# Loading a projection's first weights by whole rows, with the first activation pieces of one row each

## The chip, the cores and the metric

One core of one Trainium2 chip. The metric is the device time of one execution in microseconds (us). Matmuls run on TensorE (PE, with its weight loads shown as PEld), elementwise work on VectorE (DVE) and ScalarE (ACT), and SyncE (SP) issues most of the DMA transfers. In every execution listed with its span, the device time was about 1.7 us over the span of the profile (first to last instruction), so spans and times can be compared by differences.

All runs here count as "fast" (within 1.5% of the fastest of the same kernel).

## The reference

Two attention blocks read the same x (2048 tokens, 1024 channels) and are mixed by a gate. Only the first lines of block A matter here:

```
qkv = x @ A_wqkv                       # 1024 -> 3 x 1024
phi = lambda t: where(t > 0, t + 1, exp(t)) + 1e-6
pq, pk = phi(q), phi(k)                # the kernel computes pk first
... linear attention A, windowed attention B, out = g * a + (1 - g) * b
```

## The kernel before

The first stage computes the keys of A. Their weights are the middle 1024 columns of A_wqkv: 1024 rows, or 8 "row tiles" of 128 rows (index `kt`). x is transposed by DMA into `xT`, also by row tile. A "row" below means such a row tile. A matmul takes 128 tokens of one row of xT and 512 columns of the weights. The first four token tiles (t = 0 to 3) times two column halves fill eight accumulator tiles in PSUM (the kernel calls them banks) and are accumulated together, so that work can begin when the first rows have arrived.

```python
WkA = [wpool.tile([P, KT, 512], BF16, name=f"WkA{h}", tag="wa") for h in range(2)]

def load_xT(k, t0, t1):          # rows 2k and 2k+1
    nc.sync.dma_start_transpose(out=xT[:, 2*k:2*k+2, t0*P:t1*P],
                                in_=rows(x, t0*P, t1*P)[:, 2*k*P:(2*k+2)*P])
def load_wk(eng, k, h):          # rows 2k and 2k+1, half the columns: 1 KB runs
    eng.dma_start(out=WkA[h][:, 2*k:2*k+2, :], in_=A_wqkv[...])

load_wk(nc.scalar, 0, 0)
nc.scalar.activation(out=first_act[:], in_=ones[:, 0:1], func=ACT.Exp)
load_wk(nc.scalar, 0, 1)
load_xT(0, 0, 2)
load_xT(0, 2, 4)
for k in range(1, 4):
    load_wk(nc.sync, k, 0)
    load_xT(k, 0, 4)
    load_wk(nc.sync, k, 1)
# ... (cut: xT for token tiles 4 to 15, xrow, the later weights)

warm_up(37)                      # 37 matmuls on constants, 128 columns each
first = [bank_k(i) for i in range(8)]
for k in range(4):
    for half in range(2):
        for t in range(4):
            for kt in (2*k, 2*k + 1):
                project(first[4*half + t], t, kt, half)
            if k == 3:
                phi(work, pk[:, t, half*512:(half+1)*512], first[4*half + t])
# ... (cut: token tiles 4 to 15, eight rows at a time; the second stage, g_ps; all the rest)
```

Note when weights are needed. Within a group of two rows the first 8 matmuls use half 0 alone, so the group's second piece of weights is needed 8 matmuls after its first.

The softmax here doesn't subtract the row's maximum and nothing guards it: scores larger than these inputs give would overflow.

## Time and profile before

| | before |
|---|---|
| median of 6 runs | 473.12 us (472.91 to 473.46) |
| span of the profiled run | 471.7 us |
| TensorE busy | 467.6 us, 99% |
| last warm-up matmul issued | 4.63 us |
| first projection matmul | 5.39 us |
| second stage's first matmul | 60.92 us |

The page's part 1 (busy time and share of each engine) and part 4 (the chain of work that ended last), kernel before:

```profile
PE 467.6 (99%) x5765; PEld 251.1 (53%) x5765; DVE 278.4 (59%) x602; ACT 168.7 (36%) x272; POOL 15.3 (3%) x30
...
PE 98%; DMA 1%; DVE 0%; issue 0%; DVEq 0%
```

TensorE is the bottleneck nearly everywhere; the one other thing on the chain is the first x piece.

The timeline of TensorE over the first 14 us, kernel before (start, duration, engine, line, what, count, and in brackets the idle time before it and what ended it):

```profile
0.84 4.10 PE L175 MATMUL warm<-const-bfloat16-1.0 128*128 128x128 bf16 x37 [0.84 <-PEq L641]
5.39 8.86 PE L169 MATMUL pk_ps<-WkA,xT 128*128 128x512 bf16 x39 [0.45 <-DMA xT<-in_A_x_dram]
```

From 5.39 on, TensorE is never without work. Ends of matmuls are modelled, so I count gaps between starts: the last warm-up is issued at 4.63, the warm-ups are 0.107 us apart, so the array could have taken a new matmul at 4.74 and stood still until 5.39.

Busy time in stretches of 2 us, kernel before (stretch, length, then busy us and number of instructions of each engine, granted clock, DMA share, GB/s):

```profile
4.00:6.00 2.00, 1.55 (x11) 0.95 (x10) 0.00 (x0) 0.00 (x0) 0.00 (x0) 1.00 1.06 248
6.00:8.00 2.00, 2.00 (x10) 0.88 (x9) 0.00 (x0) 0.00 (x0) 0.00 (x0) 1.00 1.01 219
8.00:10.00 2.00, 2.00 (x11) 0.90 (x10) 0.00 (x0) 0.00 (x0) 0.64 (x2) 1.00 1.16 271
```

The number to read is the count of PE instructions. At full clock these matmuls start 0.216 us apart, so 2 us hold 9 or 10 starts.

### The profile page before, as it was taken

What the parts mean: (1) busy time and instruction counts of PE and PEld (TensorE: products, weight loads), DVE (VectorE), ACT (ScalarE), POOL (GpSimd) and SP (SyncE); (2) the same over time, 40 slices, a digit from 0 to 9 for tenths busy, and PEclk for the clock granted to TensorE, in tenths of its full rate; (3) what the DMA queues carried; (4) which work ended last, traced back from release to release, by engine and by line L of the source; (5) the groups of instructions that cost most, each with busy time, mean ns of one, the idle gap of its engine ahead of it and who ended that gap; (6) DMA issues with size and microseconds to landing.
All of it is one profiled execution on the core that took longest, in us unless ns stands there. A gap on an engine that the chain in (4) does not pass through costs nothing.

```text
span 471.7 us, 13176 instructions
## 1 busy us (share of the span) xinstructions
PE 467.6 (99%) x5765; PEld 251.1 (53%) x5765; DVE 278.4 (59%) x602; ACT 168.7 (36%) x272; POOL 15.3 (3%) x30
## 2 busy tenths in 40 slices
PE   8999999999999999999999999999999999999997
PEld 5444444445444444445677777777764444444444
DVE  0586689990329999999567676767670049800000
ACT  1343321112443333333555555555551134221121
POOL 3300000500000000000000000000000000000000
PEclk9999999999999999999999999999999999999999
DMA  8999970000643233627326364632563913221101
GB/s 220 193 246 374 348 248 0 0 1 1 213 134 108 92 142 128 156 96 248 103 56 100 71 91 96 91 93 63 93 173 67 227 64 79 69 54 45 35 33 46
DMA packets 98732, 55.40 MB, mean 117 GB/s; under 512 B 70130, under 2 KB 90610, under 8 KB 98674
## 3 DMA queue, kind: packets, MB, share of 16 engines
q1 hardware_dynamic: 93378, 49.87, 41.1%
q10 hardware_dynamic: 5296, 4.69, 2.9%
q8 instruction: 45, 0.74, 0.7%
q14 instruction: 13, 0.11, 0.1%
HBM read 26.10 MB, written 15.86 MB: 89 GB/s over the span
## 4 chain that ended last, share of the span: by engine, by line
PE 98%; DMA 1%; DVE 0%; issue 0%; DVEq 0%
PE q_ps L388 27%; PE d_ps L592 12%; PE p_ps L295 12%; PE pk_ps L169 12%; PE g_ps L220 12%; PE e_ps L592 12%; PE p_ps L331 9%; PE po L467 2%; PE s2b L445 2%; DMA xT<-in_A_x_dram 1%; PE kv_ps L240 0%; PE w_ps L283 0%; DVE osb L599 0%; DVEq L599 0%
## 5 line engine op out<-in xcount | busy, mean ns | idle before, releaser
L388 PE MATMUL q_ps<-xT,WqB 64*64 64x512 bf16 x1024 | 69.7, 377 | 0.0
L388 PE MATMUL q_ps<-xT,WkB 64*64 64x512 bf16 x1024 | 69.0, 376 | 0.0
L156 DVE TENSOR_SCALAR e<-e 128x512 f32<-128x512 f32 x64 | 27.1, 423 | 64.0 <-ACT e L155 64.0
L295 PE MATMUL p_ps<-WvB,xT 128*128 128x512 bf16 x256 | 57.9, 379 | 0.0
L169 PE MATMUL pk_ps<-WkA,xT 128*128 128x512 bf16 x256 | 55.7, 380 | 0.4 <-DMA xT<-in_A_x_dram 0.4
L220 PE MATMUL g_ps<-pk,xrow 128*128 128x512 bf16 x256 | 55.4, 379 | 0.0
L450 ACT ACTIVATE PT<-s2b 128x928 bf16<-128x928 f32 (+4 forms) x40 | 34.1, 854 | 45.5 <-PE s2b L445 45.5
L452 DVE TENSOR_TENSOR PT<-PT,mask 128x928 bf16<-128x928 bf16 (+4 forms) x40 | 23.6, 589 | 36.2 <-ACT PT L450 36.2
L331 PE MATMUL p_ps<-WqA,xT 128*128 128x512 bf16 x192 | 43.4, 379 | 0.0
L592 PEld LDWEIGHTS <-pqT 128*128 128x128 bf16 x272 | 26.0, 98 | 29.8 <-issue 0.4
L592 PEld LDWEIGHTS <-OBT 128*128 128x128 bf16 x272 | 26.0, 98 | 29.4
L169 PEld LDWEIGHTS <-xT 128*128 128x128 bf16 x256 | 25.0, 98 | 30.9 <-DMA xT<-in_A_x_dram 0.7
L220 PEld LDWEIGHTS <-xrow 128*128 128x128 bf16 x256 | 25.0, 98 | 30.2
L295 PEld LDWEIGHTS <-xT 128*128 128x128 bf16 x256 | 24.6, 98 | 30.0 <-issue 0.9
L388 PEld LDWEIGHTS <-WkB 64*64 64x64 bf16 x1024 | 34.0, 107 | 11.6 <-issue 0.4
L388 PEld LDWEIGHTS <-WqB 64*64 64x64 bf16 x1024 | 32.5, 107 | 11.1 <-issue 1.0
L599 DVE TENSOR_SCALAR osb<-e_ps,omg 128x128 bf16<-128x128 f32 x1 | 0.4, 351 | 57.6 <-PE e_ps L592 57.6
L155 ACT ACTIVATE e<-pk_ps 128x512 f32<-128x512 f32 x32 | 18.9, 597 | 40.5 <-PE pk_ps L169 36.3
L300 ACT CAST tmp<-p_ps 128x512 bf16<-128x512 f32 x32 | 18.7, 589 | 37.1 <-PE p_ps L295 32.3
L592 PE MATMUL d_ps<-WoA,pqT 128*128 128x512 bf16 (+1 forms) x136 | 30.9, 370 | 0.0
L331 PEld LDWEIGHTS <-xT 128*128 128x128 bf16 x192 | 18.8, 98 | 22.6
L592 PE MATMUL d_ps<-WoB,OBT 128*128 128x512 bf16 (+1 forms) x136 | 30.8, 370 | 0.0
(63 smaller groups left out, 530.3 us busy)
## 6 DMA issues: line engine op xcount, KB each, us to landing
vd<-tmp SPq DMA_DIRECT2D x16, 264.0 KB
xrow<-in_A_x_dram SPq DMA_DIRECT2D x4, 1024.0 KB
out_dram<-osb ACTq DMA_DIRECT2D x31, 128.0 KB
pqd<-tmp SPq DMA_DIRECT2D x12, 256.0 KB
WvA<-in_A_wqkv_dram SPq DMA_DIRECT2D x2, 1024.0 KB
WoA<-in_A_wo_dram SPq DMA_DIRECT2D x2, 1024.0 KB
WvB<-in_B_wqkv_dram SPq DMA_DIRECT2D x2, 1024.0 KB
WqA<-in_A_wqkv_dram SPq DMA_DIRECT2D x2, 1024.0 KB
```

What stands on the lines that cost most here:

```text
L155: nc.scalar.activation(out=e[:], in_=pj[:], func=ACT.Exp)
L156: nc.vector.tensor_scalar(out=e[:], in0=e[:], scalar1=1.0, scalar2=1e-6, op0=ALU.min, op1=ALU.add)
L169: nc.tensor.matmul(pj[:], lhsT=xT[:, kt, t * P:(t + 1) * P], rhs=WkA[half][:, kt, :], start=(kt == 0), stop=(kt == KT - 1))
L220: nc.tensor.matmul(pj[:], lhsT=xrow[:, t, kt * P:(kt + 1) * P], rhs=pk[:, t, half * 512:(half + 1) * 512], start=(t == 0), stop=(t == NB - 1))
L295: nc.tensor.matmul(st["pj"][:], lhsT=xT[:, kt, t * P:(t + 1) * P], rhs=WvB[half][:, kt, :], start=(kt == 0), stop=(kt == KT - 1))
L300: nc.scalar.copy(out=v[:, half * 16:(half + 1) * 16, 0:Dh], in_=st["pj"][:].rearrange("p (h e) -> p h e", h=16))
L331: nc.tensor.matmul(st["pj"][:], lhsT=xT[:, kt, t * P:(t + 1) * P], rhs=WqA[half][:, kt, :], start=(kt == 0), stop=(kt == KT - 1))
L388: nc.tensor.matmul(banks[o][64 * j:64 * j + 64, :], lhsT=lhsT(r, kt, j), rhs=rhs(r, kt), start=first and kt == 0, stop=kt == KT - 1, skip_ ...
L445: nc.tensor.matmul(s2b[64 * par:64 * par + 64, pair, :, o:o + w], lhsT=kts[c][r, par, k0:k0 + 64], rhs=qz[r, :, par, q0 % 512:q0 % 512 + w ...
L450: nc.scalar.activation(out=pt[:, :, 0:W_], in_=s2b[:].rearrange("p a b s -> p (a b) s")[:, :, 0:W_], func=ACT.Exp, scale=SCALE)
L452: nc.vector.tensor_tensor(out=pt[:, :, 0:W_], in0=pt[:, :, 0:W_], in1=mask[:, None, base:base + W_].broadcast_to([P, 4, W_]), op=ALU.mult)
L592: nc.tensor.matmul(st["ps"][:, 0:n], lhsT=lhsT, rhs=W[c0 // 512][:, c, c0 % 512:c0 % 512 + n], start=(side == 0 and c == 0), stop=(side == ...
```

## The change

Its intent: longer runs (2 KB for 1 KB) for the key weights, smaller first pieces of x in rows, and an order of matmuls that starts with one row over all eight banks. Core of the diff (the same edit of WqA's and lw's tiles is cut; TensorE's, VectorE's and GpSimd's instructions keep their order and number, apart from the rows' order in the first 64 matmuls):

```diff
-    WkA = [wpool.tile([P, KT, 512], BF16, name=f"WkA{h}", tag="wa") for h in range(2)]
+    WkA = wide.tile([P, KT, D], BF16, name="WkA", tag="wa")
...
+    def load_wk(eng, kt):
+        eng.dma_start(out=WkA[:, kt, :], in_=A_wqkv[kt * P:(kt + 1) * P, D:2 * D])
...
-        load_wk(nc.scalar, 0, 0)
-        first_act = consts.tile([P, 1], BF16, name="first_act")
-        nc.scalar.activation(out=first_act[:], in_=ones[:, 0:1], func=ACT.Exp)
-        load_wk(nc.scalar, 0, 1)
-        load_xT(0, 0, 2)
-        load_xT(0, 2, 4)
-        for k in range(1, 4):
-            load_wk(nc.sync, k, 0)
-            load_xT(k, 0, 4)
-            load_wk(nc.sync, k, 1)
+        load_wk(nc.scalar, 0)
+        load_wk(nc.scalar, 1)
+        load_xT(0, 1, 0, 4)
+        load_xT(1, 1, 0, 4)
+        for kt in range(2, KT, 2):
+            load_wk(nc.sync, kt)
+            load_xT(kt, 2, 0, 4)
+            load_wk(nc.sync, kt + 1)
...
-            for k in range(4):
+            for kts_ in ((0,), (1,), (2, 3), (4, 5), (6, 7)):
                 for half in range(2):
                     for t in range(4):
-                        for kt in (2 * k, 2 * k + 1):
+                        for kt in kts_:
                             project(first[4 * half + t], t, kt, half)
-                        if k == 3:
+                        if kts_[-1] == KT - 1:
```

More of the change, by code (lines that the diff above doesn't have):

```diff
@@ L71 @@
     wpool = ctx.enter_context(tc.tile_pool(name="wpool", bufs=2))
+    wide = ctx.enter_context(tc.tile_pool(name="wide", bufs=1))
     dram = ctx.enter_context(tc.tile_pool(name="dram", bufs=1, space=bass.MemoryType.DRAM))
@@ L89, in load_rows, with load_xT @@
         eng.dma_start(out=xrow[:, t0:t1, :], in_=rows(x, t0 * P, t1 * P).rearrange("(t p) d -> p t d", p=P))
-    WkA = [wpool.tile([P, KT, 512], BF16, name=f"WkA{h}", tag="wa") for h in range(2)]
-    def load_xT(k, t0, t1):
-        nc.sync.dma_start_transpose(out=xT[:, 2 * k:2 * k + 2, t0 * P:t1 * P],
-                                    in_=rows(x, t0 * P, t1 * P)[:, 2 * k * P:(2 * k + 2) * P])
-    def load_wk(eng, k, h):
-        eng.dma_start(out=WkA[h][:, 2 * k:2 * k + 2, :],
-                      in_=A_wqkv[2 * k * P:(2 * k + 2) * P, D + 512 * h:D + 512 * h + 512]
-                      .rearrange("(kt p) n -> p kt n", p=P))
+    WkA = wide.tile([P, KT, D], BF16, name="WkA", tag="wa")
+    def load_xT(kt, n, t0, t1):
+        nc.sync.dma_start_transpose(out=xT[:, kt:kt + n, t0 * P:t1 * P],
+                                    in_=rows(x, t0 * P, t1 * P)[:, kt * P:(kt + n) * P])
+    def load_wk(eng, kt):
+        eng.dma_start(out=WkA[:, kt, :], in_=A_wqkv[kt * P:(kt + 1) * P, D:2 * D])
     ones = nc.const_aps.tensor(1.0, [P, P], BF16)
     with tc.manual_schedule(engines={SP, mybir.EngineType.Activation}):
-        load_wk(nc.scalar, 0, 0)
-        first_act = consts.tile([P, 1], BF16, name="first_act")
-        nc.scalar.activation(out=first_act[:], in_=ones[:, 0:1], func=ACT.Exp)
-        load_wk(nc.scalar, 0, 1)
-        load_xT(0, 0, 2)
-        load_xT(0, 2, 4)
-        for k in range(1, 4):
-            load_wk(nc.sync, k, 0)
-            load_xT(k, 0, 4)
-            load_wk(nc.sync, k, 1)
+        load_wk(nc.scalar, 0)
[6 more added lines that the diff above has]
+            load_wk(nc.sync, kt + 1)
         for t in range(4, NB):
@@ L122 @@
         WvB = load_w("WvB", B_wqkv, 2 * D, "wc")
-    WqA = load_w("WqA", A_wqkv, 0, "wa")
+    WqA = wide.tile([P, KT, D], BF16, name="WqA", tag="wa")
+    for h in range(2):
+        nc.sync.dma_start(out=WqA[:, 4 * h:4 * h + 4, :],
+                          in_=A_wqkv[512 * h:512 * h + 512, 0:D].rearrange("(kt p) n -> p kt n", p=P))
     mask = consts.tile([P, S // 2], BF16, name="mask")
@@ L168, in project @@
             def project(pj, t, kt, half):
-                nc.tensor.matmul(pj[:], lhsT=xT[:, kt, t * P:(t + 1) * P], rhs=WkA[half][:, kt, :],
+                nc.tensor.matmul(pj[:], lhsT=xT[:, kt, t * P:(t + 1) * P], rhs=WkA[:, kt, half * 512:half * 512 + 512],
                                  start=(kt == 0), stop=(kt == KT - 1))
@@ L330, in mm @@
                         st["pj"] = bank()
-                    nc.tensor.matmul(st["pj"][:], lhsT=xT[:, kt, t * P:(t + 1) * P], rhs=WqA[half][:, kt, :],
+                    nc.tensor.matmul(st["pj"][:], lhsT=xT[:, kt, t * P:(t + 1) * P], rhs=WqA[:, kt, half * 512:half * 512 + 512],
                                      start=(kt == 0), stop=(kt == KT - 1))
@@ L544 @@
             fw = wpool.tile([P, 2, D], F32, name="fw", tag="wc")
-            lw = wpool.tile([P, 4, D], BF16, name="lw", tag="wa")
+            lw = wide.tile([P, 4, D], BF16, name="lw", tag="wa")
             def qa_output(t, half):
@@ L551, in rhs @@
                 def rhs(r, kt):
-                    return WqA[half][64 * r:64 * r + 64, kt, :]
+                    return WqA[64 * r:64 * r + 64, kt, half * 512:half * 512 + 512]
                 def evacuate(ps, part):
```

## The prediction

> **What bounds the kernel now.** TensorE. The page has PE busy 467.6 of 471.7 us (99%); its chain of waits is 98% PE, 1% DMA (the x pieces). In the trace the projection matmuls start 0.216 us apart from the third on, without a hole. Only the start is unused: the last of 37 warm-up matmuls (0.107 us apart) is issued at 4.63, so the first real one could start at about 4.75; it starts at 5.39, after 0.45 us idle that the waits put on the DMA of xT. Only this start, and new holes in the first 16 us, can move the time.
>
> **What the change does.** The same work on every engine in the same order, apart from the order of the first 64 matmuls and one removed 0.20 us activation off the chain. Bytes are unchanged. WkA goes from eight DMAs with 1 KB rows to eight with 2 KB rows (256 KB each). In this trace a 1 KB packet takes 46 ns, a 2 KB one 84 ns: per engine 16 x 46 = 0.74 us or 8 x 84 = 0.67 us a piece, an estimated gain of 0.06 us. The first matmul still needs 256 KB of weights and 128 KB of x. In before the first two pieces of WkA landed at 3.74 and 4.99, the first two of x at 5.34 and 5.56; the first x piece had moved its packets by about 3.7, but its completion came after the second weight piece's packets. [...] So the four stay coupled, and x row 0 lands at about 5.1.
>
> An earlier start is worth about half: the first two matmuls were 0.399 and 0.310 us apart, and the clock record shows full clock from 5.97 us. [...] A start at 4.75 would gain 0.3 us, at 5.1 about 0.15 us.
>
> **What it adds.** In before, a group's second half of weights was needed 8 matmuls (1.7 us) after the first. Now both rows of a group are needed by its second matmul. The piece in row 3's place landed at 9.14; row 3 is needed at about 9.0 to 9.1. Row 5: 12.2 against 12.5; row 7: 14.8 against 15.9. So a stall of 0 to 0.3 us before rows 2 and 3, which 2 KB packets may shorten; nothing later. WqA and lw have tens of microseconds of slack.
>
> **Prediction.** 472.8 us, 80% range 472.1 to 473.6: -0.2 us, inside 2%. Chances: faster by over 2% 0.01, within 2% 0.98, slower by over 2% 0.01.
>
> **Right if** the first projection matmul starts between 4.75 and 5.4, still after a wait for xT; at most one hole, under 0.3 us, before matmul 17 or 18, waiting on WkA; everything later shifted by 0.0 to 0.4 us at the same spacing. **Wrong if** the first start is after 5.5, holes over 0.5 us stand at rows 1, 3, 5 or 7, or a later stage has PE idle that before does not have.
>
> **What would make it wrong.** One-row transposes (256 bytes wide in the source) that issue or move more slowly; larger weight packets taking a bigger share of the engines, so that x lands later; full clock coming later; a wait for the whole weight tile rather than its row.

(That work runs at about half rate before full clock rests there on the spacing of matmuls, 0.399 and 0.310 us for 0.216 later, and the coupling on the landing times alone; both are measured below.)

## The result

| | before | changed |
|---|---|---|
| median of 6 runs | 473.12 us | 473.28 us |
| all six | 472.91 to 473.46 | 473.16, 473.24, 473.25, 473.32, 475.00, 475.57 |
| profiled run | 473.39 us | 475.00 us |
| first projection matmul, profiled run | 5.39 us | 5.76 us |
| full clock from, profiled run | 5.97 us | 9.26 us |

The ratio of changed to before is 1.0016 (0.9995 to 1.0037). Ratios are the mean time of one kernel's fast runs over the mean of the other's of the same rounds, so not quite the ratio of the medians quoted. The verdict is "same" at 2%, as predicted. But four runs are 0.1 us slower by the median and two are 2 us slower, and the trace fell on one of the two. So its differences must be read as those of a late run.

The same parts of the page, and its clock row from part 2, changed kernel:

```profile
PE 467.0 (99%) x5734; PEld 250.2 (53%) x5765; DVE 278.5 (59%) x602; ACT 168.6 (36%) x271; POOL 15.3 (3%) x30
...
PEclk9999999999999999999999999999999999999999
...
PE 98%; DMA 1%; issue 0%; DVE 0%; DVEq 0%
```

TensorE's busy share and the chain's shares are the same (31 matmul records are missing from this trace). The page's row of the granted clock in 40 slices shows nothing unusual either.

Timeline of TensorE, changed kernel, first 14 us:

```profile
0.84 4.10 PE L175 MATMUL warm<-const-bfloat16-1.0 128*128 128x128 bf16 x37 [0.84 <-PEq L641]
5.76 8.58 PE L169 MATMUL pk_ps<-WkA,xT 128*128 128x512 bf16 x30 [0.82 <-DMA xT<-in_A_x_dram]
```

The stretches, changed kernel:

```profile
4.00:6.00 2.00, 1.18 (x10) 0.80 (x9) 0.00 (x0) 0.00 (x0) 0.00 (x0) 1.00 1.06 218
6.00:8.00 2.00, 2.00 (x6) 0.74 (x5) 0.00 (x0) 0.00 (x0) 0.00 (x0) 1.00 1.15 249
8.00:10.00 2.00, 2.00 (x8) 0.77 (x7) 0.00 (x0) 0.00 (x0) 0.25 (x2) 1.00 1.16 288
```

Between 6 and 8 us TensorE is busy all 2.00 us in both kernels, but it holds 6 matmuls and not 10. In the trace they start 0.427 us apart until 9.14: half clock. The clock column says 1.00 here and is wrong. The trace's clock record has no entry before full clock was first granted (5.97 in before, 9.26 in the changed kernel), and a stretch without an entry is shown as 1.00. At the start of a kernel the spacing of equal matmuls tells the clock, not that column.

This sum closes. Time to the second stage = start + half of the time spent at half clock + holes + a constant:

| | before | changed (late run) | difference |
|---|---|---|---|
| start of the first projection matmul | 5.39 | 5.76 | +0.37 |
| half of (full clock - start) | 0.29 | 1.75 | +1.46 |
| rest, up to the second stage's first matmul | 55.24 | 55.23 | -0.01 |
| second stage's first matmul | 60.92 | 62.73 | +1.81 |
| from there to the end | 410.74 | 410.54 | -0.20 |

Across the 18 other traces, the "rest" is 55.22 to 55.26 in every one where TensorE has no hole, and the last line 410.5 to 410.8 in all but one (411.25). So whatever the change does to the time, it does before about 10 us: a later start, a later full clock, or a hole.

### The profile page after: what moved, and what is told of

The parts are those of the page before. It is cut to its first block, busy times and chain, and to the rows that moved or that the text cites. A ratio compares the mean times of both kernels' runs of the same rounds, so it can differ in the third digit from the quotient of the medians.

```text
span 473.3 us, 13143 instructions
## 1 busy us (share of the span) xinstructions
PE 467.0 (99%) x5734; PEld 250.2 (53%) x5765; DVE 278.5 (59%) x602; ACT 168.6 (36%) x271; POOL 15.3 (3%) x30
## 4 chain that ended last, share of the span: by engine, by line
PE 98%; DMA 1%; issue 0%; DVE 0%; DVEq 0%
PE q_ps L388 27%; PE pk_ps L169 12%; PE d_ps L592 12%; PE p_ps L295 12%; PE g_ps L220 12%; PE e_ps L592 11%; PE p_ps L331 9%; PE po L467 2%; PE s2b L445 2%; DMA xT<-in_A_x_dram 1%; PE kv_ps L240 0%; PE w_ps L283 0%; DVE osb L599 0%; DVEq L599 0%
## 5 line engine op out<-in xcount | busy, mean ns | idle before, releaser
L388 PE MATMUL q_ps<-xT,WqB 64*64 64x512 bf16 x1024 | 69.4, 377 | 0.0
L388 PE MATMUL q_ps<-xT,WkB 64*64 64x512 bf16 x1024 | 68.9, 376 | 0.0
L169 PE MATMUL pk_ps<-WkA,xT 128*128 128x512 bf16 x251 | 56.9, 387 | 1.1 <-DMA xT<-in_A_x_dram 0.8
L388 PEld LDWEIGHTS <-WkB 64*64 64x64 bf16 x1024 | 33.3, 107 | 12.2 <-issue 0.4
L388 PEld LDWEIGHTS <-WqB 64*64 64x64 bf16 x1024 | 32.1, 107 | 11.1 <-issue 0.7
```

The lines of the kernel that those rows point to most:

```text
L169: nc.tensor.matmul(pj[:], lhsT=xT[:, kt, t * P:(t + 1) * P], rhs=WkA[:, kt, half * 512:half * 512 + 512], start=(kt == 0), stop=(kt == KT ...
L388: nc.tensor.matmul(banks[o][64 * j:64 * j + 64, :], lhsT=lhsT(r, kt, j), rhs=rhs(r, kt), start=first and kt == 0, stop=kt == KT - 1, skip_ ...
```

## The experiments

Two theories. **Late clock:** the 2 us come from the clock. A longer idle gap between warm-up and first projection matmul (1.02 us for 0.65 in the first two traces) makes full clock come later (9.26 us for 5.97), and TensorE works at half clock until then (matmuls 0.427 us apart for 0.216). **Late data alone:** runs are slow because data come late, by the lateness of the data; warm-ups don't matter.

The table lists every run, with the median of its executions (5 or 6, one of them the profiled one), the late runs among them, and its trace. "Before" is the median of the not-late runs of the kernel before on the same chip in the same call. "Hole" is time between two projection matmuls beyond their spacing. At 2% every run is "same" (the largest ratio, of actall, is 1.0073), so all differences below are smaller than that.

| run | median us | late | before | start | full clock | hole |
|---|---|---|---|---|---|---|
| again (changed) | 473.35 | 1 of 6 | 473.06 | 5.80 | 5.19 | 0 |
| warm43 | 473.72 | 0 of 6 | 473.06 | 5.99 | 5.61 | 0 |
| warm31 | 474.98 | 5 of 6 | 473.06 | 5.68 | 10.25 | 0 |
| xrows | 473.39 | 1 of 6 | 473.06 | 5.96 | 3.84 | 0 |
| before2 (before) | 473.12 | 1 of 5 | 473.05 | 5.42 | 4.25 | 0 |
| xpairs | 473.50 | 1 of 6 | 473.05 | 5.96 | 3.78 | 0 |
| wk1sp | 474.27 | see text | 473.05 | 4.74 | 6.13 | 1.3 |
| again2 (changed) | 473.69 | 0 of 5 | 473.05 | 5.32 | 5.56 | 0.73 |
| wk2late | 473.21 | 0 of 6 | 473.06 | 5.63 | 4.40 | 0 |
| actall | 476.84 | see text | 473.06 | 5.12 | 5.34, 15.59 | 3.2 |
| wkb2late | 473.14 | 0 of 6 | 473.06 | 5.48 | 5.76 | 0 |
| warm40 | 472.86 | 0 of 6 | 473.06 | 5.38 | 5.11 | 0 |
| b43 | 473.19 | 0 of 6 | 473.11 | 5.63 | 4.03 | 0 |
| xrows43 | 473.52 | 0 of 6 | 473.11 | 6.08 | 6.22 | 0 |
| xpairs43 | 473.51 | 0 of 6 | 473.11 | 5.35 | 4.15 | 0.32 |
| rows43 | 473.76 | 0 of 6 | 473.11 | 5.62 | 3.61 | 0.52 |
| rows23 | 473.42 | 0 of 6 | 473.21 | 5.75 | 5.02 | 0 |
| warm40b | 473.17 | 0 of 6 | 473.21 | 5.54 | 4.72 | 0 |

All outputs were correct.

### The clock: more and fewer warm-up matmuls

**again**: the changed kernel unedited.

> The changed kernel once more, for more executions. Theory (late clock): the times fall in two groups, about 473.2 us (full clock from about 6 us) and about 475.2 us (full clock only about 3.3 us later, since TensorE idled about 1.0 us instead of 0.65 us between warm-up and first projection matmul); in the trace a start before about 5.5 us goes with the fast group, one after about 5.6 us with the slow one. Rival (late data alone): the times are spread evenly with the start of the first matmul, by at most its delay of 0.4 us, and the 475 us runs have holes in TensorE instead.

One of six runs was late (475.15), the others 473.02 to 473.71. The trace refutes one detail of what I expected: it starts at 5.80, later than the late run's 5.76, and yet is not late. Full clock came at 5.19. So the start alone doesn't decide: here full clock had come 0.61 us before it.

**warm43**: the changed kernel with a longer warm-up.

```diff
-            warm_up(37)
+            warm_up(43)
```

> The changed kernel with 43 warm-up matmuls for 37, which end at about 5.4 us: the idle gap is filled and nothing else differs. Late clock: no run near 475 us; all within 0.4 us of 473.2, full clock near 6 us in the trace. Late data alone: two groups as in the changed kernel, a third of the runs 2 us slower.

No late run. The spread (473.33 to 474.12) is a little wider than expected, and the start of the trace is the second latest of all, 5.99: late data, but no late clock.

**warm31**: the kernel before, loads and all, with a shorter warm-up.

```diff
-            warm_up(37)
+            warm_up(31)
```

> The kernel before with 31 warm-up matmuls for 37: loads and data arrival untouched, TensorE idles about 1.3 us before the first projection matmul. Late clock: most or all runs at 475.0 to 475.6 us, full clock about 3.3 us later than in before. Late data alone: the same time as before, 473.1, since the first matmul still waits for the same x piece.

Five of six runs are late (474.61 to 475.55), one is not (472.94). Its timeline, and then its stretches:

```profile
0.84 3.46 PE L175 MATMUL warm<-const-bfloat16-1.0 128*128 128x128 bf16 x31 [0.84 <-PEq L641]
5.68 8.67 PE L169 MATMUL pk_ps<-WkA,xT 128*128 128x512 bf16 x28 [1.38 <-DMA xT<-in_A_x_dram]
```

```profile
6.00:8.00 2.00, 2.00 (x6) 0.76 (x5) 0.00 (x0) 0.00 (x0) 0.00 (x0) 1.00 1.08 240
8.00:10.00 2.00, 2.00 (x6) 0.68 (x5) 0.00 (x0) 0.00 (x0) 0.62 (x2) 1.00 1.10 277
```

Six matmuls in each 2 us until full clock at 10.25. The loads are those of before, so late data cannot be the reason. This run settles it for late clock. warm43 agrees, but its 0 of 6 alone would prove little, since the changed kernel has 3 late runs in 17 (below).

The record of granted full clock lasts 467.626 us in every trace that is not late (actall, below, apart) and 464.213 us in the only two late runs that were traced: a difference of 3.413 us. The two are 137 and 136 times 3.4133, and in actall full clock lasts 6.83 us (5.34 to 12.17) and the half clock after it 3.41, two times and one. So in these traces the clock changes in steps of 3.413 us. (For the other late runs, the late clock is inferred from their time.) In the traces that are not late full clock comes anywhere from 3.61 to 6.22 us, so the steps have no fixed place in the kernel.

How busy was TensorE before full clock? In each trace I took the step of 3.413 us up to full clock, and the one before that, and subtracted the time when no matmul was being issued. Steps that ended in full clock: 78% (wkb2late), 80% (xrows43), 81% (before) and more. Steps that did not: 76% (warm31, from 0.01 to 3.42), 70% (changed kernel's late run, from 2.43 to 5.84), 54% (warm31, the next one) and less. So I estimate a limit between 76% and 78% here, an idle time of about 0.75 to 0.82 us in a step. Each end of this rests on a single step, and that the busy share of the step decides is my inference from these shares. From 4.74 to a start at 5.39 is 0.65 us; to 5.76 it is 1.02 us. By this estimate a start later than about 5.5 is late if the whole gap falls in one step before full clock. It was harmless where full clock had come before the gap ended, as in "again" (full clock at 5.19, start at 5.80).

**warm40** and **warm40b**: the kernel before with 40 warm-ups, twice.

> The kernel before with 40 warm-up matmuls for 37 (they end at 5.06 us, idle gap 0.3 to 0.6 us). Late-clock model: no slow run near 475, the others unchanged at 472.8 to 473.4. With late data alone: like before, now and then a run near 475.

> The kernel before with 40 warm-up matmuls, repeated: no run near 475, median 472.8 to 473.1, i.e. 0.0 to 0.3 us below before in the same call. If 472.86 was luck of that chip: the same as before's fast runs within 0.1 us.

No late run in 12, medians 472.86 and 473.17 against 473.06 and 473.21 for before's not-late runs. The second expectation's upper limit (473.1) was missed. The gain of the median is not shown, since the ratios are 0.9994 (0.9979 to 1.0009) and 0.9989 (0.9972 to 1.0007).

The eight variants with 40 or 43 warm-ups gave no late run in 48. The kernel before with 37 gave 7 in 66 (3 of 11 on one chip), and the changed kernel 3 in 17. So the kernel before has the late runs too; its first six happened to have none. That the change makes them more frequent is not shown by 3 in 17 against 7 in 66.

**before2** and **again2**: both kernels once more on one chip.

> The kernel before once more, for its spread and a second trace. By the late-clock model (span = 465.9 us + start of the first projection matmul + half of the time from there to full clock): a start between 5.3 and 5.7 us, most runs 472.7 to 473.9[...].

> The changed kernel a third time, beside before on the same chip, for the share of slow runs and a third start time. Late-clock model: start 5.6 to 6.0 us; [...] so 1 to 4 of 6 slow near 475, the rest 473.0 to 473.7.

(The model's 465.9 us is the span less the start and half of the time to full clock in the first two traces: 465.99 and 465.77.)

Before: 472.95 to 473.28 and one at 474.98; start 5.42. Changed: 473.68 to 474.01, none late, which is outside the 1 to 4 that I expected, and start 5.32, the earliest of the changed kernel. And yet it is 0.6 us slower than before. Its timeline shows why:

```profile
5.32 3.94 PE L169 MATMUL pk_ps<-WkA,xT 128*128 128x512 bf16 x16 [0.37 <-DMA xT<-in_A_x_dram]
9.82 4.48 PE L169 MATMUL pk_ps<-WkA,xT 128*128 128x512 bf16 x20 [0.56 <-DMA WkA<-in_A_wqkv_dram]
```

The second line is a new wait: after rows 0 and 1 TensorE does one matmul of row 2 and then waits for row 3 of the weights, which landed at 9.78. Start to start the hole is 0.73 us. In before, the piece in that place landed at 9.14 and was needed only 8 matmuls later. The early start is not the whole reason: in the other two traces of the changed kernel row 3 landed at 8.94 and 9.11. With 9.11 this hole would have been near zero.

### Which part makes it later

**xrows**: before, with only the x pieces and the matmul order of the change. **xpairs**: the changed kernel with the x pieces and the matmul order of before, so weights by whole rows alone.

```diff
 # xrows, against before (the helper's new arguments are cut)
-        load_xT(0, 0, 2)
-        load_xT(0, 2, 4)
+        load_xT(0, 1, 0, 4)
+        load_xT(1, 1, 0, 4)
-            for k in range(4):
+            for kts_ in ((0,), (1,), (2, 3), (4, 5), (6, 7)):
 # xpairs, against the changed kernel
-        load_xT(0, 1, 0, 4)
-        load_xT(1, 1, 0, 4)
+        load_xT(0, 2, 0, 2)
+        load_xT(0, 2, 2, 4)
-            for kts_ in ((0,), (1,), (2, 3), (4, 5), (6, 7)):
+            for kts_ in ((0, 1), (2, 3), (4, 5), (6, 7)):
```

> The kernel before with only the x pieces of one row and the order of the first 64 matmuls of the change; key weights by half rows as before. If one-row x pieces are what lands late: two groups of times, some near 475. If the 2 KB weight rows are: all runs near 473.1, like before.

> The changed kernel with the x pieces and the matmul order of before (two pieces of two rows by two token tiles), key weights by whole rows as changed. If the one-row x pieces are what makes the start late: a start near 5.4 us, fast runs at about 473.0. If the 2 KB weight rows are: a start near 5.75, fast runs at 473.3 and slow ones at 475. The first matmul pair now needs weight rows 0 and 1, which landed at 5.3 to 5.6 with the changed kernel, so this start cannot be much before 5.4.

Each part alone started at 5.96 in its trace, with one late run in six and medians 0.33 and 0.45 us over before's. Neither could be named, and late runs blur the times. So the same four corners were run with 43 warm-ups:

> The kernel before with 43 warm-up matmuls: the baseline of four corners without slow runs. Expected 472.8 to 473.2 median, no run near 475, start 5.4 to 5.6.

> Before with one-row x pieces and their matmul order, 43 warm-up matmuls. If the x part makes the start late: 0.3 to 0.5 us over before with 43, start 5.7 to 6.0. If the weight rows do: within 0.1 us of before with 43.

> The changed kernel with x pieces and order of before (weights by whole rows alone), 43 warm-up matmuls. If the weight part makes the start late: 0.3 to 0.5 us over before with 43. If only the x part does: within 0.1 us. A possible third cause, that the first matmul pair needs both weight rows, gives a start bound by weight row 1 and not by x.

Medians: 473.19 before, 473.52 with the x part, 473.51 with the weight part, on one chip. (The whole change with 43, warm43, was 473.72 on another chip, 0.66 over its before.) Each part alone costs about 0.3 us by the medians of six, though the ranges overlap (473.03 to 473.56, 473.40 to 473.86, 473.18 to 473.91). In the one trace of each they do it differently: xrows43 starts late, at 6.08. xpairs43 starts at 5.35 but waits 0.32 us for weight row 3 at 8.82. Its time after the second stage's start is also the one odd value, 411.25 for 410.5 to 410.8: TensorE's waits show one idle time of 0.5 us at q_ps (L388), for which the profile names no cause. So by what way the weight part costs its 0.3 us is not shown.

### The hole before rows 2 and 3

**rows43**: the changed kernel with 43 warm-ups and all rows singly; **rows23**: the same with only rows 2 and 3 singly.

```diff
-            for kts_ in ((0,), (1,), (2, 3), (4, 5), (6, 7)):
+            for kts_ in tuple((kt,) for kt in range(KT)):                # rows43
+            for kts_ in ((0,), (1,), (2,), (3,), (4, 5), (6, 7)):        # rows23
```

> The changed kernel with 43 warm-up matmuls and every weight row a group of its own, so that row 3 is needed 8 matmuls after row 2 and not right behind it. The earlier run of the changed kernel with 43 measured 473.33 to 474.12. If holes before rows 2 and 3 are part of the loss: less spread and 0.1 to 0.4 us below that, no hole in the trace. If only the late start counts: 473.3 to 474.1 again.

> The changed kernel with 43 warm-up matmuls, rows 2 and 3 taken singly, rows 4 to 7 in pairs as changed. If the hole before rows 2 and 3 was part of the loss: no hole there and none at the first stage's end, median 473.2 to 473.5, below the 473.74 of the changed kernel with 43 and the 473.76 of all rows singly. If the late start is all: 473.6 to 473.8 again.

rows43 had no hole at rows 2 and 3 but gained nothing (473.76), because my edit made another one, at 19.23. TensorE's waits in its first 24 us name it:

```profile
PE pk_ps L169 <- DMA xT<-in_A_x_dram: 0.9, 1, 0.9
...
PE pk_ps L169 <- DVE pk L157: 0.4, 1, 0.4
```

With the last row as its own group the eight banks finish within 1.7 us, and VectorE, which needs 0.43 + 0.69 us for each, doesn't free them in time. rows23 avoids both. It had no hole, and with 473.42 it is 0.2 us over its before, where warm43 and rows43 are 0.65 us over theirs. That would fit the hole as a part of the loss, but it is not shown: the traced run of warm43 (473.70) has no hole at these rows, only the late start of 5.99. The chips differ too, and two of the six runs of rows23 were still at 473.89 and 474.02.

### Where the late x piece comes from

**wk1sp**: the changed kernel with weight row 1 moved behind the first x piece on SyncE's queue.

```diff
-        load_wk(nc.scalar, 1)
         load_xT(0, 1, 0, 4)
+        load_wk(nc.sync, 1)
         load_xT(1, 1, 0, 4)
```

> The changed kernel with weight row 1 moved from ScalarE's queue to SyncE's, behind the first x piece. If the first x piece's completion waits for the packets and writes of the second weight piece [...]: it lands at 4.2 to 4.6 us, the first projection matmul starts at the end of warm-up, 4.75 us, no gap, no slow run, median 472.5 to 472.8. If the x piece is late for its own reasons (one-row transposes are slow): start unchanged near 5.75 and slow runs remain. At most a hole of 0.3 us before the row 1 matmuls, since x row 1 is issued 0.6 us later.

The x piece landed at 3.96 to 4.15 (its 16 completions), against 4.74 to 5.71 in the changed kernel's first trace, and the first projection matmul started right after warm-up. Its data packets were no earlier (the 512th of 256 bytes began at 3.66, against 3.56). So the coupling is shown: the x piece's completion is held up by the second weight piece on the other queue. All other traces agree: in 19 of 19 the x piece landed after that weight piece, by 0.22 to 0.63 us, in 15 of them by 0.29 to 0.43. By what mechanism is not shown. But the time got worse, by 0.6 us over again2. Its timeline:

```profile
4.74 4.73 PE L169 MATMUL pk_ps<-WkA,xT 128*128 128x512 bf16 x16
10.42 3.83 PE L169 MATMUL pk_ps<-WkA,xT 128*128 128x512 bf16 x17 [0.94 <-DMA WkA<-in_A_wqkv_dram]
```

No idle time before the start, and all of it given back, and more, waiting for weight row 3, which landed at 10.38 where again2 had 9.78. That is the edit's own doing: with row 1 on its queue SyncE issued row 3 at 5.92, for 5.33 in again2. By the sum above, wk1sp against again2 has -0.58 us from the start, +0.58 from half clock (full clock came only at 6.13) and +0.6 from the holes. (So the traced run, 474.56, is over 474.4 us for its holes, 1.12 us at 9.08 and 0.2 us at 8.67, and not for a late clock. The other run over that line has no trace.) An early start is worth nothing when the next rows don't come earlier.

DMA throughput in the stretches shows a dip before the start. First the changed kernel, then wk1sp:

```profile
3.60:4.20 0.60, 0.60 (x8) 0.60 (x7) 0.00 (x0) 0.00 (x0) 0.00 (x0) 1.00 1.03 366
4.20:4.80 0.60, 0.60 (x7) 0.47 (x5) 0.00 (x0) 0.00 (x0) 0.00 (x0) 1.00 1.58 198
4.80:5.20 0.40, 0.14 (x2) 0.00 (x0) 0.00 (x0) 0.00 (x0) 0.00 (x0) 1.00 0.53 73
```

```profile
3.60:4.20 0.60, 0.60 (x8) 0.60 (x7) 0.00 (x0) 0.00 (x0) 0.00 (x0) 1.00 0.70 120
4.20:4.80 0.60, 0.60 (x8) 0.60 (x7) 0.00 (x0) 0.00 (x0) 0.00 (x0) 1.00 0.84 253
4.80:5.20 0.40, 0.40 (x4) 0.12 (x2) 0.00 (x0) 0.00 (x0) 0.00 (x0) 1.00 1.20 258
```

In the changed kernel the last column falls to 73 GB/s around 5 us, when the first weight copy behind transposes on SyncE's queue begins (weight row 2). In wk1sp, where a weight copy follows the first transpose, a fall to 120 GB/s comes at 3.6 to 4.2. That is a coincidence in time, which the next runs test.

**wk2late** and **wkb2late** move that copy behind the next transpose, in the changed kernel and in the kernel before.

```diff
-            load_wk(nc.sync, kt)
             load_xT(kt, 2, 0, 4)
+            load_wk(nc.sync, kt)
             load_wk(nc.sync, kt + 1)
```

> The changed kernel with weight row 2 issued behind the x piece of rows 2 and 3 instead of ahead of it (and rows 4, 6 likewise). [...] If that switch is the cause of the late start: the dip moves past the third x piece, the first x piece lands at 4.8 to 5.2, start near 5.1, fast runs 472.7 to 473.1 unless a hole before rows 2 and 3 gives it back (row 2 is issued 1.3 us later, so a hole of 0.3 to 1 us there is likely). If the dip comes from elsewhere: start unchanged at 5.3 to 6.0.

> The kernel before with each group's x piece ahead of its first half of weights. Same reasoning as for the changed kernel with row 2 late; here the second half of a group is needed 8 matmuls after the first, so the hole should be smaller: start near 5.1, hole 0 to 0.5 us before rows 2 and 3, 472.7 to 473.2. If the dip is not the switch: start at 5.4 to 5.7 as in before, 473.1.

The dip was shallower in the first (165 GB/s at 4.8 to 5.2, against 66 to 143 in three traces of the changed kernel, and 163 at 5.2 to 5.8). In the second it stayed: 117 at 4.8 to 5.2, against 108 and 143 in two traces of before, although the first weight copy on SyncE's queue now began only at 6.16. The start did not come earlier, at 5.63 and 5.48 for the expected 5.1. In wk2late 14 of the 16 completions of the first x piece landed by 5.30 and two at 5.58 and 5.59. Medians of 473.21 and 473.14 are within 0.15 us of before. So the switch from transpose to copy is not shown to cause the dip, wkb2late speaks against it, and what holds the last completions up is open.

**actall** puts all weight rows on ScalarE's queue, so that SyncE's has transposes alone.

```diff
-            load_wk(nc.sync, kt)
+            load_wk(nc.scalar, kt)
             load_xT(kt, 2, 0, 4)
-            load_wk(nc.sync, kt + 1)
+            load_wk(nc.scalar, kt + 1)
```

> The changed kernel with all eight weight rows on ScalarE's queue, SyncE's first transfers being x pieces only. If switching between transposes and copies within one queue costs the dips: no dips, rows 2 and 3 land well before 8.9, no hole there; but [...] the start may be as late as 5.5 to 6. Expected 472.8 to 473.5. If the dips come from transposes and copies being on the engines at all: dips remain, time like the changed kernel, 473.3 to 474.

Far off: 476.24 to 477.66. The dip at 4.8 to 5.2 us is gone (164 GB/s follow at 5.2 to 5.8), and the first x piece landed at 5.07, earlier than in any trace of the changed kernel. But a longer dip comes later, with transposes alone on SyncE's queue and weight copies on ScalarE's:

```profile
4.80:5.20 0.40, 0.23 (x3) 0.09 (x2) 0.00 (x0) 0.00 (x0) 0.00 (x0) 1.00 1.09 250
...
8.00:10.00 2.00, 1.03 (x4) 0.39 (x4) 0.00 (x0) 0.00 (x0) 0.00 (x0) 1.00 1.08 81
```

Weight row 3 was issued only at 6.59 and landed at 12.08. TensorE waited for it, and after the wait it ran at half clock for 3.41 us. A line of its waits, and then its stretches:

```profile
PE pk_ps L169 <- DMA WkA<-in_A_wqkv_dram: 3.1, 1, 3.1
```

```profile
10.00:12.00 2.00, 0.00 (x0) 0.00 (x0) 0.00 (x0) 0.00 (x0) 1.46 (x4) 1.00 0.78 163
12.00:14.00 2.00, 1.87 (x5) 0.69 (x5) 0.00 (x0) 0.00 (x0) 1.94 (x6) 0.54 1.19 307
14.00:16.00 2.00, 2.00 (x7) 0.72 (x6) 0.00 (x0) 0.00 (x0) 1.89 (x5) 0.60 1.21 288
16.00:18.00 2.00, 2.00 (x11) 0.93 (x10) 0.00 (x0) 0.00 (x0) 1.53 (x8) 1.00 1.18 319
```

Here the clock column does show it (0.54, 0.60), since there is an entry from 12.17 to 15.59. The cost is a hole of 3.2 us plus half of 3.41 us. The late issue has a cause in the trace: the instruction waits for the semaphore of the second x piece, which landed at 6.57. Both DMAs have that semaphore, and row 3 needs no x, so this looks like the reuse of a semaphore; no run tests it.

## Why the prediction was right or wrong

**Right.** The bottleneck, and that only the first 16 us could change. The coupling: the x piece's completion waits for the second weight piece (wk1sp: landing about 4.1 when that piece is moved). The packets: in the first 16 us a 1 KB weight packet took 46 ns (median, before) and a 2 KB one 84 ns (changed). That the class is "same". That WqA and lw have slack: the time from the second stage on is no longer (410.54 us, before 410.74).

By its own test the prediction is wrong all the same: it named a first start after 5.5 us as a failure, and the traced start is 5.76 (5.80 and 5.32 in the two later traces).

**Wrong, first step: "x row 0 lands at about 5.1".** It landed at 5.71 in the first trace of the changed kernel, 5.75 in the second and 5.27 in the third (5.34 in before). I took the 0.06 us per piece saved on packets as a saving on the landing. The packets did move as said, but the landing is set by the last of 16 completions (in the first trace they came from 4.74 to 5.71). The last data packet of the first two weight pieces began at 4.25 us in the mean of six traces with the changed loads, for 4.43 in six with before's; yet the second of these pieces landed at 5.30, for 5.07. The x piece comes behind it, so the delay is there already. In the first trace the x piece's data packets had begun by 3.6 and its completion packets by 4.22, and the last of these landed at 5.71. DMA throughput was at its lowest in between. Instead of a start 0.25 us earlier, six traces with the changed loads (after, again, again2, warm43, rows43, rows23; "after" is the first result) start at 5.71 in the mean (5.32 to 5.99), and six with before's loads (before, before2, warm31, warm40, warm40b, b43) at 5.51 (5.38 to 5.68): later by 0.2 us, with more scatter, and the two ranges overlap. What is shown is that the gain of 0.25 us did not come. Each half of the change alone costs about 0.3 us (xrows43, xpairs43), so neither is the culprit by itself; the cause on the DMA side stays open.

**Wrong, second step: "the clock record shows full clock from 5.97 us".** I used that as a fixed point of the kernel, and sized an early or late start at half its value from it. It was one draw: 5.97, 4.25, 5.11 and 4.72 in four traces with before's loads and 37 or 40 warm-ups. In the late run the gap of 1.02 us was 30% of the 3.413 us up to 5.84, and full clock came one step later, at 9.26; in before the gap of 0.65 us was 19% of the step up to 5.97, where full clock came. (By the estimate above the limit is 22 to 24%.) A step of 3.41 us at half clock costs half of it, 1.7 us. Start and clock together I had at about -0.15 us; in the late run they measured +1.83 us, of which the clock is 1.46. Late runs pulled the changed kernel's mean of six to 473.92 us, above my range, while its median of 473.28 lies inside. Shown by warm31 (5 of 6 late with before's loads); warm43 (none with the changed ones) agrees.

**Undersized: "a stall of 0 to 0.3 us before rows 2 and 3".** Right in place and cause, but 0.73 us in one of three traces of the changed kernel and 0 in the other two. It came with the early start (5.32) and was absent with the late ones (5.76, 5.80): weight row 3 is the next limit, at about 9 to 9.8 us. Most of the 0.73 us is row 3 landing later there (9.78, for 8.94 and 9.11), for a reason that stays open. But the prediction treated start and stall as two independent terms, and they trade against each other: a start earlier by some time only lengthens the wait for a row that lands no earlier, as in wk1sp.

## What to carry to other kernels

A short idle gap between warm-up and first real work can cost more than its own length: here a gap 0.37 us longer went with full clock 3.29 us later and cost 1.83 us. So make the warm-up long enough to meet late data, not the usual data. With three extra warm-up matmuls (0.3 us) there was no late run in 12, at no visible cost; 12 are few against 7 in 66, but all eight variants with three or six extra ones had none in 48. When data arrive in a chain, ask what the next pieces' deadlines are before buying an earlier start, and run a kernel often enough to see whether its times have two groups before one trace of it is explained.

## What these runs show of the clock and the DMA queues

- Before full clock, steps of 3.413 us with matmuls being issued 78% of the time (wkb2late) ended in it, 76% (warm31) did not. A gap of 1.02 us (the changed kernel's late run) went with a delay by one step, a cost of 1.7 us (half of 3.41). After full clock had been granted, a gap of 1.6 us (xrows: last warm-up issued at 4.29, start at 5.96) left it open, while a hole of 3.2 us (actall) was followed by half clock for 3.41 us.
- The late clock is 0.4% of the time, and yet the largest difference between runs, 473 against 475 us, in 7 of 66 runs of the kernel before.
- DMA throughput dips with transposes and plain copies under way: from 366 GB/s to 73 GB/s around 5 us in the changed kernel. The dip is not tied to a switch from transposes to copies on one queue: wkb2late has it (117 GB/s) before its first such copy, and actall has 250 GB/s at 4.8 to 5.2 us but 81 GB/s from 8 to 10 us. The runs here don't compare the speed of transposes with that of plain copies, and don't separate the cause of the dip.
- Issuing on two queues has a cost here: a piece on the other queue held up the x piece's completion by 0.8 to 1.6 us (wk1sp against the changed kernel's first trace: 3.96 to 4.15 against 4.74 to 5.71).
